# Cross-covariance attention and mixture of adapters: v of batch 0 loaded in two parts per tile, each at its own place among the loads

## Chip, cores and metric

One core of one Trainium2 chip. The metric is device time in microseconds; lower is better. The kernel before takes 256.3 us (median of 3 runs, 256.26 to 256.34).

## What is computed

Inputs are q, k and v of 4 batches x 6400 rows x 256 columns in float32 (26.2 MB each), and a small router and eight rank-16 adapters. The output is 25600 x 256 float32 (26.2 MB). Cut to what matters:

```python
# attention over the channels, per batch
qn = q / (norm(q, axis=1) + 1e-6);  kn = k / (norm(k, axis=1) + 1e-6)   # norms over the 6400 rows
a  = softmax(kn.T @ qn / tau)                                            # 256 x 256
x  = v @ a                                                               # 6400 x 256
# mixture of adapters, per row of x
logits = x @ w_gate                        # 8 experts
top 2 of the 8, softmax over those two -> w
out = x + sum over the two experts e of  w_e * (x @ A[e]) @ B[e]
```

The matrix `a` of a batch needs all of that batch's q and k. v is needed only after that, row by row.

## The kernel before

**Layout.** A batch's 6400 rows are 128 partitions x 50 columns; a column is one row of 256 values per partition, so a column of one input is 128 x 256 float32, 0.131 MB in HBM. Loads are issued by POOL (`nc.gpsimd.dma_start`) and turn float32 into bfloat16 on the way, so they write half of what they read. q and k of a batch come in five tiles of ten columns each, two DMAs per tile (`qk`, L138 and L139); v of a batch comes in three tiles of 18, 16 and 16 columns (`VP`), one DMA each (`vt`, L141). There are four buffers for `qk` tiles (`QKB`) and three for `vt` tiles (`VB`).

**Phases.** Batch 0 first: for each column the Gram matrix k'q is accumulated (`gram`, L207), the squares are taken on ACT or DVE (`square`, L197, L199) and summed by matmuls (`norm`, L218, L224). Then a chain of small steps (`chain0` to `chain6`) makes the softmax matrix of the batch. After that comes one long loop over slots. A slot is a pair of columns of v: slot 0 is columns 0 and 1 of batch 0, slot 25 the first pair of batch 1, and so on up to slot 99. In a slot, PE transposes the pair (`transposes`, L354), and in the slots behind it the gating, `z_gz` (L460), `gz_t` (L484), `y_mm` (L476) and `delta` (L496) of earlier pairs follow. Between these, the Gram and norm matmuls of the next batch are dealt out over fixed ranges of slots:

```python
GRAM = {1: (0, 20), 2: (24, 45), 3: (49, 67)}
```

So batch 1's columns are consumed in slots 0 to 20, beside batch 0's v. Every engine executes its instructions in the order in which the program wrote them.

**Order of loads.** `loads` is a list of (due slot, kind, batch, tile, parts) sorted by due slot (L91 to L100). A `qk` tile is due at the slot where its first column is used; a `vt` tile at its first pair's slot plus 1. `load_more` (L120) walks this list and issues loads in exactly this order; it stops when the next tile's buffer is still in use, and it is called again in every slot. The list `left` counts the columns of each tile that have not been read, and `where` gives a tile's place in that list. Beside the buffer, an issue on POOL also waits until the DMA that was issued eight loads before it has landed, because eight semaphores go round for these loads.

**Stores.** `delta` (L500) copies finished pairs from PSUM to `ys`; when a group of pairs is done (five pairs, fewer at the end) it is put on `unsent`, and `send` (L514) issues its store of 1.31 MB from ACT once more than six groups wait (`DEFER`; this number falls to 0 after slot 67). The last ten pairs are stored one by one from SP (L503).

Of the kernel before, what the change touches and what calls it, by code (L numbers as in the profile page):

```python
# [9 lines left out]
BF16 = mybir.dt.bfloat16  # L10
# [6 lines left out]
def kernel(  # L17
# [17 lines left out]
    B, N, C = q.shape  # L35
    P = 128
    NC = N // P
# [7 lines left out]
    PC = 10  # L45
    NPAIR = NC // 2
# [3 lines left out]
    VP = [18, 16, 16]  # L50
    FIRST = 4
# [11 lines left out]
    qk_pool = ctx.enter_context(tc.tile_pool(name="qkp", bufs=QKB))  # L63
    v_pool = ctx.enter_context(tc.tile_pool(name="vp", bufs=VB))
# [17 lines left out]
    qk_need = {}  # L82
    for b, (first, last) in GRAM.items():
        n = last - first + 1
        for c in range(NC):
            s = first + c * n // NC
# [2 lines left out]


    loads = []  # L91
    for s in range(NC // PC):
        loads.append((-10 + s, "qk", 0, s, {0: [PC - FIRST], NC // PC - 1: [6, 4]}.get(s, [PC])))
        for b in range(1, B):
            loads.append((qk_need[b, s], "qk", b, s, [PC]))
    for b in range(B):
        for s, n in enumerate(VP):
            loads.append((NPAIR * b + sum(VP[:s]) // 2 + 1, "v", b, s,
                          [8, 4, 4] if b == B - 1 and s == len(VP) - 1 else [n]))
    loads.sort(key=lambda x: x[0])  # L100
    tiles = {"qk": {}, "v": {}}
    left = {"qk": [], "v": []}
    bufs = {"qk": QKB, "v": VB}
    where = {}
    at_load = [0]
# [14 lines left out]
    def load_more(limit=1000):  # L120

        while limit and at_load[0] < len(loads):
            _, kind, b, s, parts = loads[at_load[0]]
            n = len(left[kind])
            if n >= bufs[kind] and left[kind][n - bufs[kind]]:
                return
            where[kind, b, s] = n
            c0 = s * PC if kind == "qk" else sum(VP[:s])
            left[kind].append(PC if kind == "qk" else sum(parts))
            o = left[kind][-1] - sum(parts)  # L130
            if kind == "qk":
                t = qk_pool.tile([P, 2, PC, C], BF16, tag="qk", name="qk")
            else:
                t = v_pool.tile([P, max(VP), C], BF16, tag="v", name="vt")
            tiles[kind][b, s] = t
            for m in parts:
                if kind == "qk":
                    nc.gpsimd.dma_start(t[:, 0, o:o + m, :], q_v[b, :, c0 + o:c0 + o + m, :])  # L138
                    nc.gpsimd.dma_start(t[:, 1, o:o + m, :], k_v[b, :, c0 + o:c0 + o + m, :])  # L139
                else:  # L140
                    nc.gpsimd.dma_start(t[:, o:o + m, :], v_v[b, :, c0 + o:c0 + o + m, :])  # L141
                o += m
            at_load[0] += 1
            limit -= 1
# [11 lines left out]
    nc.sync.dma_start(bst, moe_B.rearrange("e r d -> (e r) d"))  # L156
    nc.sync.dma_start(ast, moe_A.rearrange("e (p cc) r -> p e (cc r)", p=P))
    load_more(3)
    ones_bf = const.tile([P, P], BF16)
    nc.vector.memset(ones_bf, 1.0)  # L160
# [4 lines left out]
    for c in range(0, FIRST, 2):  # L165
        t = tiles["qk"][0, 0]
        nc.vector.tensor_copy(t[:, 0, c:c + 2, :], stage[:, 0, c:c + 2, :])
        nc.scalar.copy(t[:, 1, c:c + 2, :], stage[:, 1, c:c + 2, :])
    load_more(1)
    ident = const.tile([P, P], BF16)  # L170
    make_identity(nc, ident)
    ident_f = const.tile([P, P], FP32)
    make_identity(nc, ident_f)
    load_more(3)

    wg_sb = const.tile([P, CC, E], BF16)
# [464 lines left out]
```

## Time and profile before

| | |
|---|---|
| runs of the kernel | 256.26, 256.30, 256.34 us; median 256.3 |
| the profiled execution | 256.33 us |
| its span | 254.5 us (so 1.8 us lie around the span) |
| mean granted TensorE clock | 0.958 |
| busy in the span | PE 220.9 us (87%), ACT 176.3 (69%), DVE 152.6 (60%), POOL 31.6 (12%) |
| bytes | HBM read 78.91 MB, written 26.21 MB |
| loads of v | 14 DMAs, 24.6 us from issue to landing (median) |

The profile is one execution. Its slices row cuts the span in 40 parts of 6.4 us; PEclk is the granted clock of TensorE in tenths, DMA the mean busy share of the core's 16 DMA engines, and GB/s what these wrote at the destination. A window row gives busy time and number of instructions of each engine, the granted clock as a share, the DMA share and GB/s. In timeline rows the first number is the start in us from the start of the span and the second the duration; the brackets give the idle time of the engine just before and what ended it. In the chain, rows are start, duration, and what the chain went through.

### The profile page before, as it was taken

To read this page: it belongs to the slowest core of one execution; us is meant where nothing else is said; L and a number is where in the kernel's file an instruction comes from. 1 tells how busy PE (TensorE), PEld (TensorE's weight loads), DVE (VectorE), ACT (ScalarE), POOL (GpSimd) and SP (SyncE) were. 2 spreads that over 40 slices of the span, in tenths; PEclk is the share of its full clock that TensorE was granted. 3 is DMA by queue.
4 is the path that set the end of the run, shared out by engine and by line. 5 is a ranking of instruction groups with operands and counts; after the bars stand their busy time and mean duration, and the time that the engine had idled before them with its cause. 6 is when DMAs were issued, how large, how long until landed. Compare 5 with 4: busy or idle time off the path is not lost.

```text
span 254.5 us, 7398 instructions
## 1 busy us (share of the span) xinstructions
PE 220.9 (87%) x3106; PEld 190.1 (75%) x3106; DVE 152.6 (60%) x577; ACT 176.3 (69%) x290; POOL 31.6 (12%) x64
## 2 busy tenths in 40 slices
PE   0787792794899999999999989999999899999990
PEld 0444461684799987998999878989998789999970
DVE  1322235345286686876867758666677677777750
ACT  2434344658178879787787797888875877877881
POOL 8131221021012010211101202000000200000000
PEclk9999998589599999999999999999999999999996
DMA  7999999999999999999999999999999999999995
GB/s 212 224 215 216 210 216 223 208 215 219 212 220 209 221 211 214 220 210 214 215 220 210 272 273 301 217 296 264 288 252 281 362 347 357 387 424 424 423 389 209
DMA packets 13746, 66.80 MB, mean 262 GB/s; under 512 B 2577, under 2 KB 2705, under 8 KB 10001
## 3 DMA queue, kind: packets, MB, share of 16 engines
q0 software_dynamic: 8064, 38.80, 74.5%
q10 hardware_dynamic: 2160, 19.66, 18.7%
q1 hardware_dynamic: 3488, 7.87, 8.5%
q8 instruction: 24, 0.39, 0.6%
q14 instruction: 10, 0.07, 0.1%
HBM read 78.91 MB, written 26.21 MB: 413 GB/s over the span
## 4 chain that ended last, share of the span: by engine, by line
PE 62%; DMA 22%; DVE 8%; ACT 3%; issue 2%; POOL 1%; DVEq 0%; POOLq 0%; ACTq 0%
PE y_ps L476 16%; DMA vt<-in_v_dram 11%; PE acc L207 11%; DMA qk<-in_k_dram 11%; PE zg L460 8%; PE y_ps L496 7%; PE vT_ps L354 7%; PE zg L484 4%; PE nrm L224 4%; PE vT_ps L375 4%; DVE gz L464 2%; ACT sq L197 1%; DVE e L406 1%; ACT ys L500 1%; DVE lm L410 1%
## 5 line engine op out<-in xcount | busy, mean ns | idle before, releaser
L197 ACT ACTIVATE sq<-qk 128x1024 bf16<-128x1024 bf16 x87 | 89.6, 1054 | 23.0 <-DMA qk<-in_k_dram 17.0
L207 PE MATMUL acc<-qk 128*128 128x256 bf16 x400 | 74.9, 288 | 14.0 <-DMA qk<-in_k_dram 7.5
L500 ACT COPY ys<-y_ps 128x512 f32<-128x512 f32 x100 | 58.8, 588 | 26.1 <-PE y_ps L496 22.6
L476 PE MATMUL y_ps<-a_bf,vT 128*128 128x256 bf16 x400 | 60.3, 273 | 0.6 <-ACT ys L500 0.6
L207 PEld LDWEIGHTS <-qk 128*128 128x128 bf16 x400 | 34.3, 102 | 24.2 <-DMA qk<-in_k_dram 10.6
L464 DVE TENSOR_TENSOR gz<-zg,gate 128x256 bf16<-128x256 f32 x100 | 41.7, 418 | 14.4 <-PE zg L460 13.0
L365 DVE COPY vT<-vT_ps 128x512 bf16<-128x512 bf16 x63 | 26.7, 424 | 31.1 <-PE vT_ps L354 30.5
L354 PE MATMUL vT_ps<-ident,vt 128*128 128x128 bf16 x400 | 39.7, 223 | 4.2 <-DMA vt<-in_v_dram 4.0
L224 PEld LDWEIGHTS <-sq 128*128 128x128 bf16 x600 | 36.4, 98 | 7.4 <-ACT sq L197 3.1
L460 PE MATMUL zg<-wa_sb,vT 128*128 128x128 bf16 x400 | 38.5, 219 | 1.2 <-DVE gzT L490 1.0
L496 PE MATMUL y_ps<-ball_sb,gzT 128*128 128x256 bf16 x200 | 38.4, 274 | 0.0
L224 PE MATMUL nrm<-ones_bf,sq 128*128 128x1 bf16 x600 | 35.9, 165 | 1.2 <-ACT sq L197 1.2
L476 PEld LDWEIGHTS <-vT 128*128 128x128 bf16 x400 | 33.6, 97 | 3.5 <-issue 0.7
L354 PEld LDWEIGHTS <-vt 128*128 128x128 bf16 x400 | 30.2, 99 | 7.0 <-DMA vt<-in_v_dram 4.6
L363 ACT COPY vT<-vT_ps 128x512 bf16<-128x512 bf16 x37 | 21.7, 588 | 10.2 <-PE vT_ps L354 8.7
L484 PE MATMUL zg<-ident,gz 128*128 128x128 bf16 x200 | 27.7, 220 | 1.1 <-DVE gz L464 0.6
L460 PEld LDWEIGHTS <-vT 128*128 128x128 bf16 x400 | 26.0, 97 | 3.3 <-issue 2.2
L138 POOL DMA_DIRECT2D qk<-in_q_dram x21 | 11.4, 545 | 112.0 <-ACT sq L197 31.0
L490 DVE COPY gzT<-zg 128x256 bf16<-128x256 bf16 x90 | 25.3, 281 | 0.0
L199 DVE TENSOR_TENSOR sq<-qk 128x1024 bf16<-128x1024 bf16 x13 | 9.0, 692 | 22.2 <-DMA qk<-in_k_dram 14.2
L484 PEld LDWEIGHTS <-gz 128*128 128x128 bf16 x200 | 15.2, 98 | 2.9 <-DVE gz L464 2.5
L496 PEld LDWEIGHTS <-gzT 128*128 128x128 bf16 x200 | 16.1, 98 | 0.4
(61 smaller groups left out, 175.1 us busy)
## 6 DMA issues: line engine op xcount, KB each, us to landing
out_dram<-ys ACTq DMA_DIRECT2D x15, 1280.0 KB, 13.3
qk<-in_q_dram POOLq DMA_DIRECT2D x18, 640.0 KB, 20.0
qk<-in_k_dram POOLq DMA_DIRECT2D x18, 640.0 KB, 23.5
vt<-in_v_dram POOLq DMA_DIRECT2D x7, 1024.0 KB, 27.7
vt<-in_v_dram POOLq DMA_DIRECT2D x4, 1152.0 KB, 24.1
out_dram<-ys SPq DMA_DIRECT2D x3, 1280.0 KB, 10.7
out_dram<-ys SPq DMA_DIRECT2D x10, 256.0 KB, 5.3
qk<-in_q_dram POOLq DMA_DIRECT2D x2, 384.0 KB, 11.0
```

The lines of the kernel that those rows point to most:

```text
L197: nc.scalar.activation(sq, src, ACT.Square)
L207: nc.tensor.matmul(acc[b][:, ic, :], t[:, 1, o, ic * P:(ic + 1) * P], t[:, 0, o, :], start=(c == 0 and ic == 0), stop=(c == NC - 1), skip_ ...
L224: nc.tensor.matmul(nrm[b][:, j:j + 1], sq[:, w, c % 2, ic * P:(ic + 1) * P], ones_bf[:, 0:1], start=(c == 0 and j == 0), stop=(c == NC - 1 ...
L354: nc.tensor.matmul(pt[:, ic, sc * P:(sc + 1) * P], vt[:, o + sc, ic * P:(ic + 1) * P], ident, is_transpose=True, start=(i == 0), stop=(i = ...
L365: nc.vector.tensor_copy(dst, src)
L460: nc.tensor.matmul(z[:, sc, :], r["vT"][:, ic, sc, :], st[b]["wa"][:, ic, E:E + ER], start=(sc == 0 and ic == 0), stop=(sc == 1 and ic == ...
L464: nc.vector.tensor_tensor(out=gz.rearrange("p c (e r) -> p c e r", e=E), in0=z.rearrange("p c (e r) -> p c e r", e=E), in1=gr["gate"][:, r ...
L476: nc.tensor.matmul(y[:, sc, :], r["vT"][:, ic, sc, :], st[b]["a"][:, ic, :], start=(sc == 0 and ic == 0), stop=False, skip_group_check=True)
L484: nc.tensor.matmul(gt[:, sc, :], r["gz"][:, sc, :], ident, is_transpose=True, start=(sc == 0), stop=(sc == 1))
L490: nc.vector.tensor_copy(gzT, gt)
L496: nc.tensor.matmul(r["y"][:, sc, :], r["gzT"][:, sc, :], ball_sb, start=False, stop=(sc == 1), skip_group_check=True)
L500: nc.scalar.copy(gr["ys"][:, r["w"]:r["w"] + 2, :], r["y"])
```

## The change

The `vt` tiles of batch 0 are no longer one load each. Each becomes two entries of the list: the first n - 8 columns, due where the whole tile was due, and the last 8 columns, due (n - 8) / 2 slots later. n is 18, 16 and 16, so the parts are 10 + 8, 8 + 8 and 8 + 8 columns. The `vt` tiles of the other batches, and all `qk` tiles, stay as they are. An entry carries its starting column `o`, and `load_more` makes the tile and counts its buffer only at the first entry of a tile. Three DMAs are added; no instruction of the other engines is added or moved, only what some of them wait for.

```diff
+        o = FIRST if s == 0 else 0
-        loads.append((-10 + s, "qk", 0, s, {0: [PC - FIRST], NC // PC - 1: [6, 4]}.get(s, [PC])))
+        loads.append((-10 + s, "qk", 0, s, o, [6, 4] if s == NC // PC - 1 else [PC - o]))
...
     for b in range(B):
         for s, n in enumerate(VP):
-            loads.append((NPAIR * b + sum(VP[:s]) // 2 + 1, "v", b, s,
-                          [8, 4, 4] if b == B - 1 and s == len(VP) - 1 else [n]))
+            at = NPAIR * b + sum(VP[:s]) // 2 + 1
+            if b == 0:
+
+                loads.append((at, "v", b, s, 0, [n - 8]))
+                loads.append((at + (n - 8) // 2, "v", b, s, n - 8, [8]))
+            else:
+                loads.append((at, "v", b, s, 0,
+                              [8, 4, 4] if b == B - 1 and s == len(VP) - 1 else [n]))
...
-            _, kind, b, s, parts = loads[at_load[0]]
-            n = len(left[kind])
-            if n >= bufs[kind] and left[kind][n - bufs[kind]]:
-                return
-            where[kind, b, s] = n
+            _, kind, b, s, o, parts = loads[at_load[0]]
+            if (kind, b, s) not in where:
+                n = len(left[kind])
+                if n >= bufs[kind] and left[kind][n - bufs[kind]]:
+                    return
+                where[kind, b, s] = n
+                left[kind].append(PC if kind == "qk" else VP[s])
...
+                tiles[kind][b, s] = t
+            t = tiles[kind][b, s]
             c0 = s * PC if kind == "qk" else sum(VP[:s])
```

The order of the loads from batch 1's first `qk` tile on, with the columns of each load of v (b, t: batch and tile):

```
before: qk(1,0)  v(0,0)[0:18]  qk(1,1)  qk(1,2)  v(0,1)[0:16]  qk(1,3)  qk(1,4)  v(0,2)[0:16]  qk(2,0)  v(1,0) ...
after:  qk(1,0)  v(0,0)[0:10]  qk(1,1)  v(0,0)[10:18]  qk(1,2)  v(0,1)[0:8]  qk(1,3)  v(0,1)[8:16]
        qk(1,4)  v(0,2)[0:8]  v(0,2)[8:16]  qk(2,0)  v(1,0) ...
```

From qk(2,0) on the order is the same.

## The prediction

> **What bounds the kernel now.** I read the slices of the span first, then a table of windows, the chain, and the tile and timeline views around single loads. v(b,t) and qk(b,s) are the tiles as loaded; slot g is the step that transposes pair g of v.
>
> ```profile
> PEclk9999998589599999999999999999999999999996
> DMA  7999999999999999999999999999999999999995
> HBM read 78.91 MB, written 26.21 MB: 413 GB/s over the span
> ```
>
> The DMA row is full from the second slice to the last but one. The windows say it more finely (the last two columns are DMA share and GB/s written at the destination; loads turn f32 into bf16, so a load's 215 GB/s is 430 read):
>
> ```profile
> 0.00:4.00 4.00, 0.00 (x0) 0.00 (x0) 0.31 (x3) 1.28 (x1) 2.97 (x10) 1.00 0.55 161
> 64.00:140.00 76.00, 74.53 (x1169) 68.14 (x1170) 52.87 (x199) 57.40 (x88) 9.54 (x18) 0.96 1.04 215
> 172.00:204.00 32.00, 30.82 (x493) 27.82 (x490) 22.97 (x91) 25.36 (x46) 2.12 (x4) 1.00 1.03 290
> 245.00:250.00 5.00, 3.00 (x30) 2.18 (x28) 1.44 (x6) 3.13 (x7) 0.00 (x0) 1.00 0.94 365
> 250.00:254.50 4.50, 0.00 (x0) 0.00 (x0) 0.00 (x0) 0.00 (x0) 0.00 (x0) 0.55 0.40 153
> ```
>
> So DMA has nearly no idle time to give: 0.45 x 4 = 1.8 us at the start, 0.06 x 5 + 0.6 x 4.5 = 3.0 us at the end, of which some 1.3 after the last landing (253.2). The 105.1 MB moved at 425 to 430 GB/s are 245 to 247 us of a span of 254.5. TensorE is the second limit: 74.5 of 76 us busy after 64. The chain alone would mislead: after 64.5 it runs on PE, and before that on one load:
>
> ```profile
> 36.03 28.47 DMA vt<-in_v_dram
> 64.54 0.61 PE vT_ps L354 x4
> ```
>
> That is v(0,1), and it is where the change works. From the tile view narrowed to each load's issue (issue + landing time) against the first reader in the timeline, the lead of a load, in us:
>
> ```
> qk(1,1) 53.45 -> 53.50  0.05     v(1,0)  93.52 -> 97.68  4.2
> qk(1,2) 59.67 -> 59.71  0.04     qk(2,1) 99.37 -> 103.6  4.2
> v(0,1)  64.50 -> 64.54  0.04     qk(3,2) 158.7 -> 163.8  5.1
> qk(1,3) 70.67 -> 72.13  1.5      v(2,1)  171.6 -> 172.3  0.7
> qk(1,4) 76.74 -> 80.26  3.5      qk(3,4) 181.4 -> 182.3  0.9
> v(0,2)  81.60 -> 83.14  1.5      v(2,2)  188.1 -> 189.7  1.7
> ```
>
> PE waits for loads up to slot 9, and nearly again at slot 59, when stores have joined the loads:
>
> ```profile
> 61.14 0.24 PE L224 MATMUL nrm<-ones_bf,sq 128*128 128x1 bf16 x4
> 64.54 0.61 PE L354 MATMUL vT_ps<-ident,vt 128*128 128x128 bf16 x4 [3.16 <-DMA vt<-in_v_dram]
> ...
> 172.33 0.39 PE L354 MATMUL vT_ps<-ident,vt 128*128 128x128 bf16 x4
> ```
> ```profile
> L141 POOL DMA_DIRECT2D vt<-in_v_dram x1: 550/550/550, 143.9 to 143.9; - x1
> DMA to landing us min/median/max: 27.7/27.7/27.7
> ```
>
> **The change, step by step.** *Bytes.* The same columns move. The order of the v and qk loads of batch 0 and 1 changes; three DMAs are added. A whole load's landing follows the one before it by 5.46 us (18 columns, 41.90 to 47.36), 4.83 (16 columns, 59.67 to 64.50) and 3.05 (10 columns, qk(1,1)): 0.30 us a column and some 0.06 over for each DMA. Three more: 0.2 us. From below: nothing. I take 0.2.
>
> Here a rule speaks against the change. The Trainium skill, "DMA: Bandwidth & Descriptors", section on the anatomy of a SWDGE DMA, gives a DMA a fixed cost of about 2.0 us beside its bytes; three added DMAs would be an estimated 6 us by it if nothing hid that cost. The spacing above shows it hidden here, as loads are queued 20 us deep.
>
> *POOL.* Each issue holds it 0.53 to 0.55 us; 12% of it is busy. An issue also waits until the DMA eight before it has landed, so with three more DMAs those behind them issue up to about three landings later. Covered: what is in flight is still seven loads of 2.4 us or more, some 17 us. If that cover went, each us of empty queue would be a us of the end.
>
> *Slots 0 to 8.* v(0,0)'s first 10 columns land 8 x 0.30 = 2.4 us before 47.36, at 44.9, so the 0.83 us wait of slot 0 (47.41) goes; qk(1,1) also lands 2.4 earlier (51.0), and its 0.38 us wait goes. The other 8 columns land after it at 53.5, read by slot 5, at 55.2 before and about 54.2 now. qk(1,2) keeps its place behind the same bytes and lands at 59.7: there PE waits some 2 us instead of 1.08. What was won so far is gone.
>
> *Slot 9.* v(0,1)'s first half lands 2.4 us earlier, 62.1. PE gets there at 61.4, waits 0.7 instead of 3.16: 2.4 us won. The clock may add to it. In the long wait it fell:
>
> ```profile
> 61.40:64.50 3.10, 0.00 (x0) 0.00 (x0) 0.23 (x2) 2.27 (x3) 0.00 (x0) 0.71 1.01 209
> 64.50:68.00 3.50, 3.46 (x32) 2.88 (x33) 1.05 (x3) 0.00 (x0) 0.53 (x1) 0.50 1.05 215
> 70.90:72.75 1.85, 1.85 (x31) 1.73 (x29) 1.81 (x10) 1.22 (x3) 0.00 (x0) 1.00 1.06 216
> ```
>
> It is half from about 62.7 to 69.5 (0.71 and 0.50 in these windows); slot 9's pass took 3.50 us, a pass at full clock 1.86 (70.89 to 72.75) or 2.17: 1.75 times. If the clock stays up, the 4.9 us from 64.54 to 69.47 shrink to 2.8, another 2.1; if it falls as before, PE spends more of the work cold and 0.8 of the 2.4 are lost. qk(1,4)'s lead caps it. So the gain G is 1.6 to 3.5 us; I take 3. The leads from slot 17 to slot 50 can carry it (v(0,2)'s first half lands 2.4 us earlier, so its 1.5 becomes 3.9; the next are 4.2).
>
> *Where G goes.* Nothing makes v(2,1), slot 59, land earlier: DMA has been full throughout, and its queue holds the same bytes ahead of it. It lands later. One store of 1.31 MB leaves each time a group of five pairs is done: ACT issues them at 139.83, 148.51, 163.09 and 172.97 (L514). They come G earlier and take about half of the DMA rate. The third, first packet at 166.48, had about 0.5 MB left when v(2,1) was through, which is 1.2 us at 428 GB/s; moved forward by 1.6 us or more, it is wholly ahead. The fourth hangs on slot 59's own pass and can't pass it. So v(2,1) lands at 171.6 + 1.2 = 172.8, PE resumes 0.5 us later than before, and on the way it stood still for G + 0.5 = 2.1 to 4.0 us, with an earlier wait of 0.04 us as the only one of its kind left.
>
> *The clock at slot 59.* A wait of 3.16 us that began at 61.38 brought the half clock after 1.3 us, for 6.8 us. A wait of 3.5 from about 169.3 should do the same: half clock till about 178.8, of which 5.9 us are PE work from 172.85, doing 5.9 / 1.75 = 3.4 us of it: 2.5 lost. If it lasts half as long, 1.1; if the clock stays, 0. The row is near, so I take 2.5. PE is then 0.5 + 2.5 = 3.0 us behind, and between 172 and 196 it had no idle time to catch up with.
>
> The Trainium skill, "TensorE: Matmul & The Clock Gate", section "Why this matters for your kernels", wants gaps over about 3 us before the clock drops. By that, G under 2.5 would leave the clock up and the end would be that of the first rival; the fall at 62.7, in a gap only 1.3 us old, says less is needed.
>
> *The end.* The last store, issued at 249.0, lands 4.2 us later behind others; the least that a store there could take is not shown. The shortest lag to a first packet in the tail is 1.7 us, transfer 0.6, landing 0.4 to 1.4: 2.7 to 3.7, so the queue covers 0.5 to 1.5 us of lateness (at worst nothing). 3.0 late less 0.7, plus 0.2 for DMAs, is 2.5 at the end, but some waits of PE at 196 to 212 (1.6 us idle) may give 0.3 back: 2.2. On the profiled run's 256.33 (span 254.5 and 1.8 around it, equal to the median 256.3): **258.5**.
>
> **The rivals.** *The stall is absorbed (same).* PE waits at slot 59 but the clock stays up, or the split loads land no earlier: 0.5 us late, 0.5 covered by the last stores' queue, 0.2 for DMAs: 256.5. For it: early waits of 1.0 to 1.7 us at 16 to 28 us left the clock at 9. Against: 62.7.
>
> *Faster.* G reaches the end. It needs the stores not to be drawn forward, or v(2,1) to land before 170, and that needs idle DMA somewhere before 170; the windows show none. The point from which it decides is slot 59: whoever starts it before 172.3 keeps that. The prize is the idle DMA in the tail, 0.3 + 1.0 us: 255.0 to 255.8, say 255.2.
>
> *The queue.* Three added DMAs and waits on the eighth before let the DMA run dry, or 4 KB pieces move worse: 0 to 2 us with no stall at slot 59 explaining it; 258.
>
> *Its own claim.* If slots 0 to 4 waited for the whole tile there would be no gain at slot 9; the instructions show slot 0 and slot 5 waiting for one DMA each, so I leave that inside the first rival.
>
> **How the numbers follow.** Forecast 0.65, 257.1 (half-length dip, most cover) to 259.5 (3.0 with no cover, plus 0.2). Absorbed 0.17, 256.2 to 256.8. Faster 0.09. Queue 0.09. 0.2% is 0.5 us, about the least that a measurement tells here; so faster 0.09, same 0.17, slower 0.74. The range, 256.1 to 259.6, leaves out the faster case and a few hundredths above, for a queue that runs dry for longer.
>
> **What would show it.** Right: slot 9's wait under 1 us and at about 62; no low PEclk digit at 64 to 70; PE waiting 2 to 4 us for vt near 169 to 173, then a PEclk digit near 5 in slice 28; slot 59 at 172.8; the last store issued near 252. Wrong: no wait at slot 59, or a wait with the clock full; DMA share under 0.9 before 240; v(2,1) landing before 171.

## The result and the profile after

The changed kernel takes 257.47 us (median of 6 runs, 257.05 to 257.65) against 256.33 us of the kernel before (6 runs, 256.26 to 256.41): slower by 0.43%, ratio 1.0043 with a 95% interval of 1.0032 to 1.0053. Timed once more beside other kernels it took 257.26 us against 256.33, ratio 1.0034 (1.0022 to 1.0045). The profiled execution took 257.05 us with a span of 255.3, 0.72 us longer than the profiled execution before. It is the shortest of the six, so the traces below account for 0.72 us and not for the whole 1.14 us between the medians.

The slices, and then the same windows as before (busy time of the engines, granted clock, DMA share, GB/s written):

```profile
PEclk9979998597999999999999999997999999999999
DMA  7999999999999999999999999999999999999995
```
```profile
64.00:140.00 76.00, 75.08 (x1224) 69.14 (x1223) 54.67 (x207) 59.79 (x92) 10.81 (x21) 1.00 1.05 216
172.00:204.00 32.00, 30.49 (x468) 27.62 (x469) 21.64 (x84) 23.65 (x44) 1.24 (x3) 0.95 1.03 283
245.00:250.00 5.00, 4.46 (x44) 3.42 (x42) 2.19 (x10) 4.02 (x11) 0.00 (x0) 1.00 1.00 386
250.00:255.30 5.30, 0.00 (x0) 0.00 (x0) 0.00 (x0) 0.42 (x1) 0.00 (x0) 0.97 0.47 182
```

The low clock of slice 11 (63.6 to 70 us) is gone (a 7 stands in slice 10 now), and a 7 stands in slice 28. DMA's busy share is what it was. From 64 to 140 PE has 0.55 us more busy time in the same 76 us, because it is ahead; from 172 to 204 it has less, and PE is still 4.46 us busy from 245 to 250, where it was 3.00 before. So a lead of PE has turned into a delay somewhere between 140 and 204. PE's timeline around slot 9 and around slot 59 tells where (start, duration; in brackets the idle time before):

```profile
61.75 0.29 PE L233 MATMUL nrm<-ones_bf,sq 128*128 128x1 bf16 x4
62.19 0.61 PE L363 MATMUL vT_ps<-ident,vt 128*128 128x128 bf16 x4
...
168.22 0.60 PE L485 MATMUL y_ps<-a_bf,vT 128*128 128x256 bf16 x4
173.12 0.61 PE L363 MATMUL vT_ps<-ident,vt 128*128 128x128 bf16 x4 [4.31 <-DMA vt<-in_v_dram]
```

Slot 9 starts at 62.19 instead of 64.54, after 0.15 us of idle time instead of 3.16. Slot 59 starts at 173.12 instead of 172.33, after 4.31 us of standing still. The load that it waits for, from the tile view of its issue, and the third store, from the same view of `out_dram`:

```profile
L150 POOL DMA_DIRECT2D vt<-in_v_dram x1: 547/547/547, 140.3 to 140.3; - x1
DMA to landing us min/median/max: 32.8/32.8/32.8
```
```profile
L523 ACTq DMA_DIRECT2D out_dram<-ys x1: 338/338/338, 159.4 to 159.4; - x1
DMA to landing us min/median/max: 13.0/13.0/13.0
```

v(2,1) is issued 3.7 us earlier than before (140.26 for 143.93) and lands 1.5 us later (173.1 for 171.6). The third store now lands at 172.4, ahead of it; before it landed at 174.4, behind it. After the wait the clock is half for 3.4 us:

```profile
168.80:173.10 4.30, 0.01 (x1) 0.00 (x0) 0.00 (x0) 0.35 (x1) 0.00 (x0) 1.00 1.03 234
173.10:176.50 3.40, 3.38 (x32) 2.81 (x33) 1.05 (x3) 1.54 (x2) 0.00 (x0) 0.50 1.06 216
176.50:180.00 3.50, 3.50 (x66) 3.29 (x65) 2.29 (x9) 2.49 (x3) 0.00 (x0) 1.00 1.04 291
```

DMA works on at 1.03 while PE stands still: PE waits for bandwidth, not for an issue. The slots' starts in the two traces give the whole account, in us after the same slot before (below zero: ahead):

```
slot            0      9      17     50     59     67     84     99    last store issued  landed
after - before -1.06  -2.35  -3.66  -3.67  +0.79  +2.28  +1.45  +1.45      +1.44          +0.75
```

### The profile page after: what moved, and what is told of

Its sections match the earlier page's. It is cut to its first block, busy times and chain, and to the rows that moved or that the text cites. A ratio compares the mean times of both kernels' runs of the same rounds, so it can differ in the third digit from the quotient of the medians.

```text
span 255.3 us, 7401 instructions
## 1 busy us (share of the span) xinstructions
PE 221.3 (87%) x3106; PEld 191.0 (75%) x3106; DVE 152.6 (60%) x577; ACT 176.4 (69%) x290; POOL 33.0 (13%) x67
## 4 chain that ended last, share of the span: by engine, by line
PE 53%; DMA 35%; DVE 5%; issue 2%; POOL 1%; ACT 1%; DVEq 0%; POOLq 0%
DMA vt<-in_v_dram 22%; PE y_ps L485 14%; DMA qk<-in_k_dram 13%; PE acc L216 8%; PE zg L469 7%; PE y_ps L505 7%; PE vT_ps L363 6%; PE zg L493 4%; PE vT_ps L384 3%; PE nrm L233 3%; DVE gz L473 1%; DVE e L415 1%; DVE lg L407 1%; DVE lm L419 1%; DVE m L411 1%
## 5 line engine op out<-in xcount | busy, mean ns | idle before, releaser
L206 ACT ACTIVATE sq<-qk 128x1024 bf16<-128x1024 bf16 x87 | 89.6, 1054 | 22.4 <-DMA qk<-in_k_dram 15.8
L150 POOL DMA_DIRECT2D vt<-in_v_dram x17 | 9.0, 534 | 69.6 <-PE y_ps L505 53.1
```

Of the source, the lines that this page charges most:

```text
L206: nc.scalar.activation(sq, src, ACT.Square)
```

## The experiments

All ran beside the kernel before, on the same chip, and are called e1 to e12 below. The kernel before took 256.44 us (median) beside e1 to e4, 256.35 beside e5, e6, e7 and e9, and 256.33 beside e8, e10, e11 and e12.

**One part of the change alone (e1, e2).**

```diff
-            if b == 0:
+            if b == 0 and s == 0:          # e1_first_only
+            if b == 0 and s == 1:          # e2_second_only
```

> Only v(0,0) is split, 10 + 8 (one added DMA); v(0,1) and v(0,2) are whole. Theory (the split gives PE a lead G at slot 9, DMA is full, so the lead is lost at slot 59 to stores drawn forward, with a clock drop): the half us won at slots 0 to 5 is lost at qk(1,2), which lands at 59.7 as before; slot 9 waits for the whole v(0,1) until about 64.5; slot 59 starts at 172.3 to 172.6; 256.2 to 256.6. Rival 1 (each added DMA and its place in the queue costs 0.38 us, a third of the 1.14 measured): 256.7. Rival 2 (the wait at qk(1,2), 2.67 us in the changed kernel, is what costs): most of the loss is here already, 257.0 or more.

Measured (e1): 256.46 us, ratio 1.0003 (0.9994 to 1.0012). The wait at qk(1,2) was 2.58 us, as long as in the changed kernel (2.67), slot 9 waited 3.20 us as before, and slot 59 started at 172.43. So neither this wait nor the first split costs anything that can be told at the end.

> Only v(0,1) is split, 8 + 8 (one added DMA). Theory: slot 9 at about 62.1 and G of 2 to 3.5 us; slot 59 stands for about G + 0.7 and starts at 172.8 to 173.2, with a clock drop; 256.9 to 257.5, nearly the whole loss with one DMA of the three. Rival 1 (per DMA): 256.7, and no wait at slot 59. Rival 2 (wait at qk(1,2)): 256.3, as that wait is 1.1 us again.

Measured (e2): 256.55 us, ratio 1.0004 (0.9996 to 1.0013): my theory's time was missed, though slot 9 came at 62.15 as expected. What I had left out is that the whole v(0,2) lands at 81.70, so most of the lead ended at slot 17:

```profile
81.75 0.40 PE L363 MATMUL vT_ps<-ident,vt 128*128 128x128 bf16 x4 [2.60 <-DMA vt<-in_v_dram]
```

PE was 4.16 us ahead of the kernel before at slot 16 and 1.39 us at slot 17; the clock was half from 83.02 to 86.44, and from slot 19 on PE was where it was before (slot 50 at 150.23, before 150.11; slot 59 at 172.44). A lead that is lost at 82 us costs nothing that can be told. The loss needs the lead to live until stores are issued, at about 136 us, and for that it seems that the third tile has to be split as well; no run splits v(0,1) and v(0,2) alone.

**The price of three more DMAs (e3).** Batch 0 whole, three later tiles split where they stand:

```diff
-            if b == 0:
-                ...
+            if (b, s) in ((2, 0), (3, 0), (3, 1)):
+                loads.append((at, "v", b, s, 0, [n - 8, 8]))
```

> Batch 0 is loaded whole as before; instead v(2,0), v(3,0) and v(3,1) are split in two parts each, at their old places (three added DMAs, leads of 5 to 11 us there). Theory: slot 9 waits 3.2 us and slot 59 starts near 172.3, as before; 256.3 to 256.6 (0.06 us for each DMA). Rival 1 (three added DMAs cost by themselves): 257.2 to 257.6.

Measured: 256.56 us, ratio 1.0005 (0.9996 to 1.0015). Three added DMAs are 0.1 us, which can't be told from nothing. Slot 59 started at 172.82 in the profiled execution, 0.49 late, but PE was as late from slot 11 on, ahead of every split. These three stand later than those of the change; e1 and e2 each have one at its place, and cost no more. So the rival of the queue falls.

**Split without new places (e7).**

```diff
-                loads.append((at + (n - 8) // 2, "v", b, s, n - 8, [8]))
+                loads.append((at, "v", b, s, n - 8, [8]))
```

> All three tiles of batch 0 split as in the changed kernel (three added DMAs), but the second part directly behind the first, so the order among the loads of q and k is that of before. Theory: v(0,1)'s first half still lands at 62.1, but qk(1,3) at 70.7 as before, where PE had 1.5 us of lead, so G is 1.5 to 2.5 instead of 3.7; the wait at slot 59 is 2 to 3 us; 256.6 to 257.3. Rival 1 (added DMAs alone): 257.5, as in the changed kernel. Rival 4 (the new places of the loads are what costs): 256.3.

Measured: 256.68 us, ratio 1.0018 (1.0007 to 1.0029). Slot 9 came at 62.11; at 70.69 PE waited 1.81 us for qk(1,3); the lead at slot 50 was 0.93 us (149.18), less than I had expected; slot 59 waited 1.14 us, where 2 to 3 were expected, and started at 172.70, 0.37 late, and the clock stayed up:

```profile
172.70 0.40 PE L363 MATMUL vT_ps<-ident,vt 128*128 128x128 bf16 x4 [1.14 <-DMA vt<-in_v_dram]
```

The time is in the expected band. With the lead at a quarter, the loss is about 0.3 us instead of 0.9 to 1.1.

**Stores against loads, in the kernel before (e4).** No split; each store one group earlier:

```diff
-    DEFER = 6
+    DEFER = 5
```

> The kernel before, with DEFER 5 for 6: each store leaves one group (about 10 us) sooner; the loads are unchanged. Theory (what is stored ahead of v(2,1) delays it byte for byte): the fourth store is then ahead of v(2,1) too, which lands 3 to 4 us later, at 175 to 176; PE waits 3 to 4 us at slot 59 with a clock drop behind it; 257.5 to 259.5. Rival 1 (the added DMAs are the cost, stores are not): 256.3, no wait over 1 us at slot 59.

Measured: 259.24 us, ratio 1.0117 (1.0101 to 1.0134). PE's timeline at slot 59:

```profile
173.06 0.60 PE L476 MATMUL y_ps<-a_bf,vT 128*128 128x256 bf16 x4
176.36 0.40 PE L354 MATMUL vT_ps<-ident,vt 128*128 128x128 bf16 x4 [2.71 <-DMA vt<-in_v_dram]
```

v(2,1) landed at 176.32, 4.7 us later than in the kernel before, with every load at its old place in the list. Up to 1.2 us of this may not be the edit's: in this execution PE was 1.2 us late from slot 11 on, long before the first store, and v(2,1) was issued as much later (so PE's wait is 2.71 us, where 3 to 4 were expected). From issue to landing it took 31.2 us instead of 27.7: what is stored ahead of v(2,1) delays it.

**The clock's share (e9).** The changed kernel with useless matmuls in place of the wait:

```diff
+        if slot == 59 and not behind:
+            junk = ps_t.tile([P, 512], FP32, tag="pt", name="junk")
+            for _ in range(36):
+                nc.tensor.matmul(junk[:, 0:256], ident, ball_sb, start=True, stop=True)
```

> The changed kernel with 36 matmuls of no use (128x256, into a spare PSUM buffer, read by nobody) on PE ahead of slot 59's transposes, some 3.9 us, so that PE is busy while it would wait. Theory: slot 59 still starts at about 173.1 (the landing is not PE's), but the clock does not drop; the 1.5 us that PE lost between slots 59 and 67 (0.8 late at slot 59, 2.3 late at slot 67) go; last store 0.5 to 1.4 us earlier: 256.4 to 257.0. If the clock has no part in it: 257.4 or more, by the filler's own work.

Measured: 256.84 us, ratio 1.0019 (1.0009 to 1.0029).

```profile
169.48 4.09 PE L593 MATMUL junk<-ball_sb,ident 128*128 128x256 bf16 x36
173.41 0.39 PE L363 MATMUL vT_ps<-ident,vt 128*128 128x128 bf16 x4
```
```profile
173.40:176.80 3.40, 3.40 (x67) 3.21 (x66) 1.57 (x5) 2.12 (x4) 0.00 (x0) 1.00 1.05 214
```

Slot 59 starts as late as in the changed kernel, but the clock is 1.00 after it, and PE does 67 matmuls in the next 3.40 us instead of 32. Slot 67 is 1.08 us late (190.81) instead of 2.28. The excess over the kernel before is 0.49 us instead of 0.93 to 1.14: the clock is about half of the loss. That the later landing is the rest is argued; PE's lead was also smaller here (2.85 us at slot 50, against 3.67), so the share is rough.

**The order near slot 59 (e8).**

```diff
-    loads.sort(key=lambda x: x[0])
+    loads.sort(key=lambda x: (x[0] - (x[1:4] == ("v", 2, 1))))
```

> The changed kernel with v(2,1) one place earlier in the list of loads, ahead of qk(3,3). Theory (bytes are the limit around slot 59, not their order): v(2,1) lands at about 167 and slot 59 starts at 168 to 170 without a long wait, but qk(3,3) then lands at about 173, where PE wants it at 170: the wait moves one slot on, 2 to 4 us; slot 67 as in the changed kernel or up to 1 us sooner; 256.4 to 257.4. Rival 5 (only the place of v(2,1) is wrong): no wait over 1 us after slot 50, 255.3 to 256.2.

Measured: 256.69 us, ratio 1.0016 (1.0008 to 1.0025). The wait moved one slot on, to qk(3,3):

```profile
168.61 0.39 PE L363 MATMUL vT_ps<-ident,vt 128*128 128x128 bf16 x4
...
173.78 0.61 PE L216 MATMUL acc<-qk 128*128 128x256 bf16 x2 [3.61 <-DMA qk<-in_k_dram]
```

Neither of the two orders serves both slots. The time is 0.6 us under the changed kernel's, and what won it isn't settled: the profiled execution took 257.14 us, 0.45 above the median of its runs, and shows slot 67 at 192.31, no earlier than there.

**Stores that make way.** Nine ys buffers and DEFER 7, with the changed and with the old loads, for all slots (e5, e6) and up to slot 65 only (e10, e11); the edits that make room for the ninth buffer are left out here:

```diff
-    QKB, VB, YB = 4, 3, 8
+    QKB, VB, YB = 4, 3, 9
-    DEFER = 6
+    DEFER = 7
...
+    # e10, e11 only:
-        send(max(0, min(DEFER, DEFER - (slot - GRAM[B - 1][1]) // 4)))
+        send(DEFER if slot < 66 else max(0, min(DEFER - 1, DEFER - 1 - (slot - GRAM[B - 1][1]) // 4)))
```

> The changed kernel with DEFER 7 for 6 and nine ys buffers for eight: each store leaves one group (about 10 us) later. For the room, five small tiles of the chain have one buffer, three of the gating have three for four, and the adapters' staging lies in the first ys tile. Theory: only two stores are ahead of v(2,1), which lands at about 169 to 170; PE, 3.6 us ahead, waits 0.5 to 1.5 us at slot 59 and the clock stays; PE keeps 2 us or more of its lead, DMA stays full, and only the idle DMA at the end can be won: 255.2 to 256.1. Rival 1 (the added DMAs cost 1.1 us wherever the stores are): 1.1 us over e6, 257.3 or so. Rival 3 (a later store is only a longer tail): 257 to 258 for both e5 and e6.

> The kernel before with the same late stores (control of e5). Theory: v(2,1) lands 1.5 to 2.5 us earlier, but PE has no lead to use it (0.7 us of slack before): slot 59 at 172.3; the end as before or, as one store more is left for the tail, a little later: 256.2 to 257.0; e5 is not slower than e6. Rival 1: e6 1.1 us below e5.

> e5 (the changed kernel with stores a group later) but only up to slot 65; from slot 66 the stores leave as in the changed kernel. Theory: slot 59 without a long wait, PE 2 us ahead at slot 67, and the store that is made up for at slot 66 goes beside v(2,2) and v(3,0), which have leads of 3 us and more; the end is DMA's, so only its idle time in the tail can be won: 255.6 to 256.4, not over e5's 256.4. Rival 3 (a lead of PE is worth its whole length at the end): 254.3 to 255.

> The kernel before with the same stores as e10 (control). Theory: 256.2 to 257.2, between the kernel before and e6 (257.4); e10 is 0.3 to 1 us below it, as e5 is below e6: the same split gains once the stores make way.

Measured: e5 256.43 us (ratio 1.0003, 0.9995 to 1.0012), e6 257.38 (1.0041, 1.0028 to 1.0054), e10 256.45 (1.0003, 0.9994 to 1.0011), e11 256.52 (1.0012, 1.0001 to 1.0022). In e5 and e10 the wait at slot 59 is gone: v(2,1) landed at 167.8 and 169.0, and slot 59 started at 170.48 and 169.51 (e5 first, then e10):

```profile
170.48 0.39 PE L365 MATMUL vT_ps<-ident,vt 128*128 128x128 bf16 x4
169.51 0.39 PE L365 MATMUL vT_ps<-ident,vt 128*128 128x128 bf16 x4
```

The split kernels are then not slower than their controls: e5 is 0.95 us below e6, and e10 is 0.07 below e11, which can't be told from nothing. So the loss of the change is not in the split but in what the stores do with the lead. But no gain over the kernel before was left either; I had expected up to 1.1 us in e5, and 0.3 to 1 us between e10 and e11. In e10 PE is 3.24 us ahead of the kernel before at slot 99 (233.17 for 236.41), and its time is the same. The windows of e10 and SP's own waits at the end show where the lead went:

```profile
240.00:245.00 5.00, 4.66 (x50) 3.71 (x47) 2.27 (x10) 4.10 (x10) 0.00 (x0) 1.00 1.00 413
245.00:250.00 5.00, 0.11 (x1) 0.00 (x0) 0.00 (x0) 0.66 (x2) 0.00 (x0) 1.00 0.78 302
```
```profile
SPq L515 <- DMA out_dram<-ys: 8.0, 2, 4.2
```

PE is done by 245, when DMA has moved, counted from the packets, as many bytes as in the kernel before and no more. The last small stores stand in line on SP, 8.0 us in all, until earlier stores have landed: SP issues at 242.88 and 247.46, just behind the landings of two of ACT's stores (242.81 and 247.39), and the last store lands at 253.4. In the kernel before these waits were 2.0 us. No run takes them away, so that they alone keep e10 from gaining is argued. Why e6 is 1 us slower than the kernel before isn't settled by a run. Counted from the packets of its trace, with loads at the bytes that they read, DMA moved 410 GB/s from 180 to 220 us there, against 425 and 419 in the two halves of that stretch before. At 210 us it was 0.43 MB behind, which at 425 GB/s is 1.0 us, as much as e6 is slower.

**The changed kernel again (e12).**

> The changed kernel as it is, beside the others on one chip: 257.1 to 257.7.

Measured: 257.26 us, with a wait of 4.25 us at slot 59 and slot 67 at 192.10.

## Why the prediction was right

The direction, the place and the mechanism held; the size came out at 1.14 us (0.93 in the second timing) where 2.2 was forecast. That the time fell in the range is a weak sign by itself: the range is 3.5 us wide and holds the whole of the rival in which the stall is absorbed. What tells them apart is slot 59.

- *Bytes and DMAs* (0.2 us): e3 measures 0.1, within noise. The estimated 6 us, which the prediction worked out from the 2.0 us a DMA in the Trainium skill, "DMA: Bandwidth & Descriptors" (anatomy of a SWDGE DMA), for the case that nothing hides that cost, are not there.
- *Slots 0 to 8*: v(0,0)'s first part landed at 44.94 (44.9 forecast), qk(1,1) at 51.02 (51.0), the second part at 53.54 (53.5), qk(1,2) at 59.69. PE was at slot 5 before its part was, waited 0.52 us, and lost all it had won in 2.67 us at qk(1,2), as was said (2).
- *Slot 9 and G*: v(0,1)'s first half at 62.14 (62.1). The wait was 0.15 us where 0.7 was forecast, as the clock was half from 60.4 to 63.8 and PE came later. G was 3.67, a little over the 1.6 to 3.5. Its size is partly luck: with the same early loads the lead at slot 50 was 3.67, 3.42, 2.85, 2.81 and 1.85 us in the traces of the changed kernel, e12, e9, e10 and e5; the half clock around slot 9 lasted 3.4 us in the first two and 6.8 us in the others. e2 shows a condition that the prediction had only touched: G lives on because v(0,2) is split too, and its first part came just in time (landed at 79.35, read at 79.48).
- *Where G goes*: v(2,1) at 173.1 (172.8), a wait of 4.31 us (2.1 to 4.0), slot 59 late by 0.79 (0.5). e4, e7 and e5 move this term up, down and away.
- *The clock at slot 59*: this is the term that was mis-sized. It was forecast at 2.5 us; slot 67 is 2.28 late after 0.79 at slot 59, so it is 1.5. The forecast's own figures don't give 2.5 either: a drop 1.3 us into a wait from 169.3 and 6.8 us of half clock end at 177.4, not at 178.8, which makes the term 2.0. Measured, the drop came at 173.07, 4.3 us into the wait, and the half clock lasted 3.4 us, not 6.8. The row that I took it from, the drop at 62.7, differs in what followed: there PE stood idle for another 1.8 us after the drop, here it worked without a break (the last section shows that this is what counts). e9 confirms the term by taking it away.
- *Catching up*: 0.3 us forecast, 0.83 measured (2.28 at slot 67, 1.45 at slot 84). PE was 1.6 us idle from 196 to 212 before, 0.9 now.
- *The end*: 1.44 late at the last store (issued at 250.4, where the prediction looked for near 252), 0.75 at its landing, so the queue covered 0.7, as forecast. The packets of the two traces, with loads at the bytes that they read, show the same lateness in another place. From 190 to 210 us DMA moved 0.35 MB less than in the kernel before, 0.8 us at 425 GB/s, and made none of it good up to 240. The first part of v(3,2), whose buffer PE frees, was issued 1.44 us late, only 0.6 us before the load ahead of it landed (2.6 before), and from 204 to 208 us DMA moved 371 GB/s instead of 418, though its busy share there was 1.01. In e9 0.12 MB are missing from 190 to 210 us, in e10 none. No run separates the two accounts.

So 0.79 + 1.49 - 0.83 - 0.69 is 0.76 us for the profiled execution (257.05 against 256.33 is 0.72). In the forecast it was 0.5 + 2.5 - 0.3 - 0.7 + 0.2. What the other executions of the changed kernel lose beyond that, up to 0.6 us, is in no trace.

Of the rivals, the absorbed stall was wrong because the clock did drop; the queue fell with e1, e2 and e3. The rival that it gets faster set its deciding point rightly, slot 59, but its prize wrongly: e10 starts slot 59 2.8 us earlier than the kernel before and wins nothing.

## What to carry to other kernels

When transfers fill the span from end to end, as here, a load that is brought forward can only move waits, and the chain of waits through the compute engine hides it: look for the next load with a small lead, and ask what the engine's head start will put into the queue in front of it. Here the head start drew stores forward, and they took the place of the very load that was next to be late. A long wait can also have a price after it: the one wait of 4.31 us cost 1.5 us of half clock, and the wait of 1.14 us in e7 none. And a full busy share of DMA is no proof of its full rate: count the bytes.

## What the runs showed of the hardware

The granted clock changes on a fixed grid. In the trace of the changed kernel its record begins at 12.64 us, and it changes at 16.05, 19.47, 43.36, 50.19, 60.43, 63.84, 173.07, 176.48 and 254.99 us: all distances are whole multiples of 3.41 us. The Trainium skill, "TensorE: Matmul & The Clock Gate", Part 1, gives a free-running window of 3413 ns, which agrees. On this grid the wait at slot 59 covers all of one window and 0.8 us of the one before; the window after it is all work, and the clock is back after one step. In the kernel before, the window after the drop at 62.7 still held 1.8 us of idle time, and the half clock lasted two steps. In the same sense the wait of 3.61 us in e8 brought a drop at 173.0 for two steps, with 0.8 us of idle time left in the first of them. How much idle time in a window is too much was not varied by any run, but the 14 traces show it. Each was cut up to 240 us into the windows of its own grid, and PE's idle time between matmul records (whose ends are modelled) was added up in each window (935 in all):

| clock in the window | idle time of PE in it | clock in the next window |
|---|---|---|
| full (869 windows) | up to 1.73 us | full, without exception |
| | 1.75 to 1.82 us | half in 4 cases, full in 2 |
| | 1.95 us and more | half, without exception (32 cases) |
| half (66 windows) | up to 0.35 us | full, without exception (36 cases) |
| | 0.51 us and more | half, without exception (30 cases) |

So about half a window of idle time brings the drop, and a window with next to none ends it. A gap of 1.81 us inside one window was enough in e7 (from 68.9 to 70.7 us), far less than the 3 us that the prediction weighed; a gap of 1.73 us in the kernel before (to 22.4 us), shared by two windows, was not.
